# Attention and MLP of one kernel in one hand-written instruction order instead of a scheduler's

## The chip, the cores and the metric

One NeuronCore of a Trainium2 chip runs the whole kernel. Its engines each work through their own list of instructions: PE (TensorE, the matmuls; PEld are its weight loads), DVE (VectorE), ACT (ScalarE), POOL (GpSimd) and SP, which only issues transfers. They wait for each other through semaphores. The metric is the device time of one execution in microseconds (us); lower is better.

## The reference

`B, H, S, D = 4, 8, 768, 48`; `x` has 3072 tokens of 384 values, `d_ff` is 2048.

```python
f = 1.0 / (1.0 + np.exp(-f_logit))
for t in range(S):
    state = f[:, :, t, :, None] * state + np.einsum('bhd,bhe->bhde', k[:, :, t], v[:, :, t])
    y[:, :, t] = np.einsum('bhd,bhde->bhe', q[:, :, t], state)
...
x = np.ascontiguousarray(attn_out.transpose(0, 2, 1, 3)).reshape(B * S, H * D)
h = x @ w_in
h2 = h * h
h3 = h2 * h
P = a[0] + a[1] * h + a[2] * h2 + a[3] * h3
Q = 1.0 + np.abs(b[0]) * np.abs(h) + np.abs(b[1]) * h2
g = P / (Q + 1e-06)
return (g @ w_out).astype(np.float32)
```

## The kernel before

The sequence is cut into 6 chunks `c` of 128 steps. A chunk has 2 units `u`, each of 2 batches with 8 heads, so there are 12 units of attention. After a chunk's two units comes its MLP on 4 x 128 = 512 tokens: 4 groups `g`, each of 4 blocks of 128 hidden values.

**A unit of attention** (`attention`): ACT makes `ef` and `ls` (log of the gate) from `fn`; PE adds them up (`cs`); ACT makes `A` and `Ai`, their exponentials; DVE makes the products `qkp` of `qn` and `kn` with them; PE transposes these (`tp`), ACT copies them out (`qkT`). PE makes the chunk's contribution to the state, `sv`, and in the same PSUM bank the logs' sums `al`; and the scores `sc`, which DVE masks (`scm`). PE adds up `y` from `scm` and from the old state. ACT copies `y` out (`ysb`); DVE renews the state from `sv` (`stmp`, then `state`), except in the last chunk; PE transposes `ysb` (`xps`), and ACT copies that into `xT`, the MLP's input.

**A group of the MLP** (`mlp`): PE makes `hp` in two halves of 12 matmuls, ACT copies each out (`hy`). DVE works on 2048 columns: `z` (absolute value), `w` and `w*z` (the denominator's part); ACT then takes the logarithm (`lq`) and an exponential (`qi`), which makes the reciprocal. DVE makes the numerator `t` in five steps and multiplies it with `qi` into `gall`. When all 4 groups of a chunk are there, PE makes `op`, 4 blocks of 16 matmuls, which ACT copies out (`osb`) and SP sends to memory.

**What sets the order**: the code lists attention and MLP of a chunk one after the other, and a scheduler orders each engine's instructions when the program is built. Each engine then keeps to its list. The transfers of `fn`, `kn` and `qn` are issued on SP, `vn` and the weights (which become bfloat16 on the way) on POOL. PSUM pools: `ps2` and `ps1` for attention, `psh` with two buffers for `hp`, `pso` for `op`.

Of the kernel before, what the change touches and what calls it, by code (L numbers as in the profile page):

```python
# [17 lines left out]
def kernel(  # L18
# [53 lines left out]
    w_pool = ctx.enter_context(tc.tile_pool(name="w_pool", bufs=1))
    a_sb = w_pool.tile([P, 4], F32, name="a_sb")
    nc.sync.dma_start(out=a_sb, in_=bass.AP(tensor=moe_a.tensor, offset=moe_a.offset,
                                            ap=[[0, P]] + list(moe_a.ap)))
    b_sb = w_pool.tile([P, 2], F32, name="b_sb")
    nc.sync.dma_start(out=b_sb, in_=bass.AP(tensor=moe_b.tensor, offset=moe_b.offset,
                                            ap=[[0, P]] + list(moe_b.ap)))
    babs = w_pool.tile([P, 2], F32, name="babs")
    nc.scalar.activation(babs, b_sb, AF.Abs)  # L80

    ld = ctx.enter_context(tc.tile_pool(name="ld", bufs=3))
    at = ctx.enter_context(tc.tile_pool(name="at", bufs=2))
# [3 lines left out]
    ps2 = ctx.enter_context(tc.tile_pool(name="ps2", bufs=1, space=PSUM))  # L87
    ps1 = ctx.enter_context(tc.tile_pool(name="ps1", bufs=1, space=PSUM))
    psh = ctx.enter_context(tc.tile_pool(name="psh", bufs=2, space=PSUM))
    pso = ctx.enter_context(tc.tile_pool(name="pso", bufs=1, space=PSUM))  # L90

    mask = consts.tile([C, C], F32, name="mask")
    make_upper_triangular(nc, mask, 1.0, diag=True)

    loaded = {}

    def load(c, u):
# [5 lines left out]
        for j in range(UB):  # L103
            b = u * UB + j
            for dst, src, eng in ((fn, f_logit, nc.sync), (kn, k, nc.sync),
                                  (qn, q, nc.sync), (vn, v, nc.gpsimd)):
                eng.dma_start(out=dst[:, j],  # L107
                              in_=src[b, :, t0:t0 + C, :].rearrange("h t d -> t h d"))
        loaded[c, u] = (fn, kn, qn, vn)

    w_sb = {}

    def load_weights():
        w_sb["in"] = w_pool.tile_from(moe_w_in.rearrange("(ko ki) n -> ki ko n", ki=P),
                                      dtype=BF16, name="w_in_sb")
        w_sb["out"] = w_pool.tile_from(moe_w_out.rearrange("(ko ki) n -> ki ko n", ki=P),
                                       dtype=BF16, name="w_out_sb")

    unit_no = [0]

    def attention(c, u, xT):

        fn, kn, qn, vn = loaded.pop((c, u))
        qk = qkp[unit_no[0] % NQK]
        ls = lsp[unit_no[0] % NQK]
        unit_no[0] += 1
        st = states[u]
        fl = "p b h d -> p (b h d)"


        ef = at.tile([C, UB, H, D], F32, name="ef")
        nc.scalar.activation(ef.rearrange(fl), fn.rearrange(fl), AF.Exp, scale=-1.0)
        nc.scalar.activation(ls[:, :, :, 0:D], ef, AF.Ln, bias=1.0)

        cs = ps2.tile([C, 2, 512], F32, name="cs", tag="w2")
        for j in range(UB):
            nc.tensor.matmul(cs[:, j, 0:DM].rearrange("p (h d) -> p h d", h=H), U, ls[:, j, :, 0:D],
                             start=True, stop=True)
        A = at.tile([C, UB, H, D], F32, name="A")
        Ai = at.tile([C, UB, H, D], F32, name="Ai")  # L140
        nc.scalar.activation(A.rearrange("p b h d -> p b (h d)"), cs[:, :, 0:DM], AF.Exp, scale=-1.0)
        nc.scalar.activation(Ai.rearrange("p b h d -> p b (h d)"), cs[:, :, 0:DM], AF.Exp, scale=1.0)
        nc.vector.tensor_mul(qk[:, :, 0, :, 0:D], qn, A)  # L143
        nc.vector.tensor_mul(qk[:, :, 1, :, 0:D], kn, Ai)

        qkT = []
        for j in range(UB):
            tp = ps1.tile([P, 2, HP, C], BF16, name="tp", tag="w1")
            for i in range(2):
                for p in range(HP):  # L150
                    nc.tensor.transpose(tp[:, i, p, :],  # L151
                                        qk[:, j, i, 2 * p:2 * p + 2, :].rearrange("t h d -> t (h d)"),
                                        ident)
            t = at.tile([P, 2, HP, C], BF16, name="qkT", bufs=4)
            nc.scalar.copy(t.rearrange("p a b c -> p (a b c)"), tp.rearrange("p a b c -> p (a b c)"))  # L155
            qkT.append(t)


        if c < NC - 1:
            sv = ps1.tile([P, 512], F32, name="sv", tag="w1")  # L160
            svv = sv[:, 0:UB * HP * D].rearrange("p (b h e) -> p b h e", b=UB, h=HP)
            al = sv[:, 448:448 + UB * HP]
            for j in range(UB):
                for p in range(HP):
                    nc.tensor.matmul(al[:, j * HP + p:j * HP + p + 1],
                                     ls[:, j, 2 * p:2 * p + 2, :].rearrange("t h d -> t (h d)"),
                                     ones, start=True, stop=True)
                    for i in range(2):
                        h = 2 * p + i
                        nc.tensor.matmul(svv[64 * i:64 * i + 64, j, p, :],  # L170
                                         qk[:, j, 1, h, :], vn[:, j, h, :],
                                         start=True, stop=True)

        scm = []
        for j in range(UB):
            sc = ps2.tile([C, 2, HP, C], F32, name="sc", tag="w2")
            for p in range(HP):
                for i in range(2):
                    r = slice(64 * i, 64 * i + D)
                    nc.tensor.matmul(sc[:, i, p, :], qkT[j][r, 1, p, :], qkT[j][r, 0, p, :],  # L180
                                     start=True, stop=True)
            m = at.tile([C, 2 * HP, C], BF16, name="scm", bufs=4)
            mb = bass.AP(tensor=mask.tensor, offset=mask.offset,
                         ap=[mask.ap[0], [0, 2 * HP], mask.ap[1]])
# [34 lines left out]
        for j in range(UB):  # L219
# [3 lines left out]
            for kk in range(KD):  # L223
                nc.tensor.transpose(xps[:, kk, :], yf[:, kk * P:(kk + 1) * P], ident)
# [46 lines left out]
    for x in order[:1]:  # L271
        load(*x)
# [42 lines left out]
```

## Time and profile before

| | |
|---|---|
| time, median of 3 runs | 471.98 us (471.62 to 473.34) |
| the profiled execution, its own time | 471.93 us |
| span of its instructions | 469.9 us |
| PE, DVE, ACT busy | 293.4, 257.8, 231.3 us |
| POOL busy | 24.9 us |

Busy times are sums over the whole span, and engines work side by side; so an engine's share says how much room there would be, and not which one sets the end. The span is what lies between the first and the last instruction; 2.03 us of the execution's time lie around it.

### The profile page before, as it was taken

The numbers are of one execution on the slowest core, as the hardware profiler recorded it, in microseconds if no ns is written. First come the engines' busy times: TensorE is split into PE (matmuls) and PEld (weight loads), VectorE is DVE, ScalarE is ACT, GpSimd is POOL, SyncE is SP. The second block draws the span as 40 slices with busy tenths as digits, with TensorE's granted clock in tenths as the row PEclk, the third lists the DMA queues.
The fourth block names the chain that finished last, engine by engine and source line by source line (L and its number), as shares of the span: only waits on it lengthen the run. The fifth ranks groups of instructions, "written<-read, shape, count | busy, mean of one in ns | idle before, by whom it ended". The sixth has DMA issues, their size and how long they took to land.

```text
span 469.9 us, 4398 instructions
## 1 busy us (share of the span) xinstructions
PE 293.4 (62%) x1744; PEld 157.4 (33%) x1744; DVE 257.8 (55%) x290; ACT 231.3 (49%) x252; POOL 24.9 (5%) x36
## 2 busy tenths in 40 slices
PE   0024596459786558786648786738786638785245
PEld 0013432235533234533324543324443225431013
DVE  3021349872239873229883229893228992229950
ACT  1214568744158734248744237744137944148431
POOL 7001000010010001010001010001000000000000
PEclk9999997657768657858656859656959657877659
DMA  9999992317260007060007160003100000000001
GB/s 141 190 159 187 178 131 39 68 33 120 66 86 0 0 1 117 35 84 0 1 1 104 49 81 4 0 0 35 50 1 0 0 0 36 35 0 0 0 17 50
DMA packets 106068, 24.65 MB, mean 52 GB/s; under 512 B 100545, under 2 KB 105665, under 8 KB 106049
## 3 DMA queue, kind: packets, MB, share of 16 engines
q1 hardware_dynamic: 78624, 18.88, 21.5%
q0 software_dynamic: 27424, 5.51, 13.4%
q8 instruction: 13, 0.21, 0.2%
q14 instruction: 7, 0.05, 0.0%
HBM read 25.17 MB, written 4.72 MB: 64 GB/s over the span
## 4 chain that ended last, share of the span: by engine, by line
PE 44%; DVE 29%; ACT 15%; SPq 6%; issue 4%; DMA 2%; DVEq 0%; ACTq 0%
PE op L262 14%; PE hp L238 11%; PE y L194 6%; SPq L107 6%; PE y L198 5%; DVE scm L185 5%; ACT hy L240 4%; DVE gall L258 4%; DVE t L254 4%; DVE w L246 3%; ACT lq L248 3%; DVE t L256 3%; PE sv L170 2%; DVE w L245 2%; DVE t L257 2%
## 5 line engine op out<-in xcount | busy, mean ns | idle before, releaser
L262 PE MATMUL op<-w_out_sb,gall 128*128 128x384 bf16 x384 | 88.7, 387 | 69.0 <-DVE gall L258 64.9
L238 PE MATMUL hp<-xT,w_in_sb 128*128 128x512 bf16 x288 | 92.1, 490 | 19.0 <-ACT hy L240 14.1
L262 PEld LDWEIGHTS <-gall 128*128 128x128 bf16 x384 | 41.1, 111 | 109.5 <-DVE gall L258 72.0
L248 ACT ACTIVATE lq<-w,one_eps 128x2048 f32<-128x2048 bf16 x24 | 48.1, 2005 | 28.1 <-DVE w L246 28.1
L240 ACT CAST hy<-hp 128x1024 bf16<-128x1024 f32 x48 | 48.1, 1007 | 24.7 <-PE hp L238 23.6
L185 DVE TENSOR_TENSOR scm<-sc,mask 128x1024 bf16<-128x1024 f32 x24 | 29.3, 1220 | 53.9 <-PE sc L180 53.8
L238 PEld LDWEIGHTS <-w_in_sb 128*128 128x128 bf16 x288 | 34.8, 121 | 70.4 <-issue 53.8
L250 ACT ACTIVATE qi<-lq 128x2048 bf16<-128x2048 f32 x24 | 46.0, 1915 | 0.3
L194 PE MATMUL y<-vn,scm 128*128 128x48 bf16 x192 | 36.9, 220 | 13.5 <-DVE scm L185 13.5
L202 ACT CAST ysb<-y 128x384 bf16<-128x384 f32 x24 | 10.3, 482 | 69.8 <-PE y L198 66.2
L243 DVE TENSOR_SCALAR z<-hy 128x2048 uint16<-128x2048 uint16 x24 | 16.5, 689 | 41.6 <-ACT hy L240 41.6
L107 POOL DMA_DIRECT2D vn<-in_v_dram x24 | 21.5, 905 | 295.9 <-PE y L198 249.2
L265 ACT COPY osb<-op 128x384 f32<-128x384 f32 x24 | 11.5, 479 | 52.1 <-PE op L262 46.2
L143 DVE TENSOR_TENSOR qkp<-qn,A 128x768 bf16<-128x768 f32 x12 | 11.5, 958 | 44.4 <-DMA qn<-in_q_dram 22.8
L198 PE MATMUL y<-state,qkT 48*128 48x48 bf16 x160 | 35.0, 219 | 0.0
L151 PE MATMUL tp<-ident,qkp 128*128 128x128 bf16 x192 | 18.8, 242 | 25.5 <-ACT qkT L155 16.1
L258 DVE TENSOR_TENSOR gall<-t,qi 128x2048 bf16<-128x2048 bf16 x24 | 29.3, 1220 | 0.6
L256 DVE TENSOR_TENSOR t<-t,hy 128x2048 bf16<-128x2048 bf16 x24 | 29.2, 1218 | 0.1
L254 DVE TENSOR_TENSOR t<-t,hy 128x2048 bf16<-128x2048 bf16 x24 | 29.2, 1217 | 0.0
L246 DVE TENSOR_TENSOR w<-w,z 128x2048 bf16<-128x2048 bf16 x24 | 29.2, 1218 | 0.0
L155 ACT COPY qkT<-tp 128x1024 bf16<-128x1024 bf16 x24 | 24.2, 1009 | 8.1 <-PE tp L151 8.0
L151 PEld LDWEIGHTS <-qkp 128*128 128x128 bf16 x192 | 14.6, 108 | 33.0 <-issue 17.1
(44 smaller groups left out, 293.3 us busy)
## 6 DMA issues: line engine op xcount, KB each, us to landing
fn<-in_f_logit_dram SPq DMA_DIRECT2D x24, 192.0 KB, 4.1
kn<-in_k_dram SPq DMA_DIRECT2D x24, 192.0 KB, 4.1
qn<-in_q_dram SPq DMA_DIRECT2D x24, 192.0 KB, 3.9
out_dram<-osb SPq DMA_DIRECT2D x24, 192.0 KB, 1.9
vn<-in_v_dram POOLq DMA_DIRECT2D x24, 96.0 KB, 3.6
w_in_sb<-in_moe_w_in_dram POOLq DMA_DIRECT2D x1, 1536.0 KB, 12.4
w_out_sb<-in_moe_w_out_dram POOLq DMA_DIRECT2D x1, 1536.0 KB, 22.4
a_sb<-in_moe_a_dram SPq DMA_DIRECT2D x1, 2.0 KB, 2.6
```

The lines of the kernel that those rows point to most:

```text
L107: eng.dma_start(out=dst[:, j], in_=src[b, :, t0:t0 + C, :].rearrange("h t d -> t h d"))
L185: nc.vector.tensor_mul(m, sc.rearrange("s i p t -> s (i p) t"), mb)
L194: nc.tensor.matmul(yv[:, i, j, p, :], scm[j][:, i * HP + p, :], vn[:, j, h, :], start=True, stop=(c == 0))
L198: nc.tensor.matmul(yv[:, i, j, p, :], qkT[j][r, 0, p, :], st[r, j, p, :], start=False, stop=True)
L238: nc.tensor.matmul(hp[:, e, :], w_in_sb[:, kk, m * P:(m + 1) * P], xT[:, kk, :], start=(kk == 0), stop=(kk == KD - 1))
L240: nc.scalar.copy(y[:, hh * 2 * NT:(hh + 1) * 2 * NT], hp.rearrange("p a n -> p (a n)"))
L246: nc.vector.tensor_mul(w, w, z)
L248: nc.scalar.activation(lq, w, AF.Ln, bias=one_eps)
L250: nc.scalar.activation(qi, lq, AF.Exp, scale=-1.0)
L254: nc.vector.tensor_mul(t, t, y)
L258: nc.vector.tensor_mul(gall[:, g * G:(g + 1) * G, :].rearrange("p a n -> p (a n)"), t, qi)
L262: nc.tensor.matmul(op, gall[:, mm, b * C:(b + 1) * C], w_out_sb[:, mm, :], start=(mm == 0), stop=(mm == KF - 1))
```

## The change

The whole body is written anew. The pieces of attention become small functions (`a_ef`, `a_cs`, ... `a_xe`), and so do those of a group (`m_h`, `m_y`, `m_q`, `m_ln`, `m_ex`, `m_p`, `m_g`, and `m_o`, `m_oe` for the output). The scheduler is switched off: each engine keeps the order in which the code names the pieces. After a first part with units 0 to 2, a loop runs over pairs of groups (`n` even and odd); in each pair stand the second half of unit `ku - 1`, the first half of unit `ku`, and two output blocks of the chunk before. The weights are now loaded as float32 on SP, into two buffers, and POOL makes them bfloat16. Several tiles have one buffer instead of two or more, `psh` among them; both `tp` halves become one, and so do the two halves of `ysb` and of `xT`.

```diff
-    psh = ctx.enter_context(tc.tile_pool(name="psh", bufs=2, space=PSUM))
+    psA = ctx.enter_context(tc.tile_pool(name="psA", bufs=1, space=PSUM))
+    psB = ctx.enter_context(tc.tile_pool(name="psB", bufs=1, space=PSUM))
+    psh = ctx.enter_context(tc.tile_pool(name="psh", bufs=1, space=PSUM))
     ps1 = ctx.enter_context(tc.tile_pool(name="ps1", bufs=1, space=PSUM))
     pso = ctx.enter_context(tc.tile_pool(name="pso", bufs=1, space=PSUM))
 
+    ctx.enter_context(tc.manual_schedule())
...
+        sv = ps1.tile([P, 512], F32, name="sv", tag="w1")
...
+            nc.vector.tensor_add(stmp, svf, stv)
+            nc.vector.tensor_mul(stv, stmp, ab)
+
+    def a_x(n):
+        s = at_[n]
+        xps = ps1.tile([P, UB, KD, C], BF16, name="xps", tag="w1")
...
+    def load_w_in(g):
+        t = wst.tile([P, KD, G * P], F32, name="wst")
+        nc.sync.dma_start(out=t, in_=moe_w_in[:, g * G * P:(g + 1) * G * P].rearrange("(ko ki) n -> ki ko n", ki=P))
+        nc.gpsimd.tensor_copy(w_in_sb[:, :, g * G * P:(g + 1) * G * P], t)
...
+    load(1)
...
+    load_w_in(0)
+    load(2)
+    for g in range(1, NG):
+        load_w_in(g)
...
+    a_T(1)
+    a_x(0)
+    a_xe(0)
+    a_Te(1)
+    load(3)
...
+    m_h(0, 0)
+    m_y(0, 0)
+    a_mul(2)
+    m_h(0, 1)
+    m_y(0, 1)
+    a_T(2)
+    m_h(1, 0)
+    a_Te(2)
+    load(4)
+    a_sc(2, 0)
+    a_sc(2, 1)
+    a_sv(2)
+    a_ef(3)
+    a_mask(2, 0)
+    a_mask(2, 1)
+    a_y(2)
+    a_cs(3)
+    load(5)
+    for g in range(NG):
+        load_w_out(g)
+
+
+    for p in range(NGR // 2):
+        ku = p + 3
+        for odd in range(2):
+            n = 2 * p + odd
...
+            m_y(n + 1, 0)
+            m_q(n)
+            if not odd:
+                if prev:
+                    a_ye(ku - 1)
+                m_h(n + 1, 1)
+                if prev:
+                    a_x(ku - 1)
+                if has:
+                    a_exp(ku)
+                if prev:
+                    a_al(ku - 1)
+                    a_xe(ku - 1)
+                m_ln(n)
+                m_ex(n)
+                m_p(n)
+                m_o(c - 1, g)
+                m_y(n + 1, 1)
+                m_h(n + 2, 0)
+                if has:
+                    a_mul(ku)
+                if prev:
+                    a_st(ku - 1)
+                m_oe(c - 1, g)
+                if has:
+                    a_T(ku)
+            else:
+                if has:
+                    a_Te(ku)
+                m_h(n + 1, 1)
+                m_ln(n)
+                m_ex(n)
+                if has:
+                    a_sc(ku, 0)
+                    a_sc(ku, 1)
+                    a_sv(ku)
+                m_p(n)
+                m_o(c - 1, g)
+                m_y(n + 1, 1)
+                m_h(n + 2, 0)
+                if has:
+                    a_mask(ku, 0)
+                    a_mask(ku, 1)
+                if ku + 1 < NUN:
+                    a_ef(ku + 1)
+                m_oe(c - 1, g)
+                if has:
+                    a_y(ku)
+                if ku + 1 < NUN:
+                    a_cs(ku + 1)
+                if ku + 3 < NUN:
+                    load(ku + 3)
+            m_g(n)
+            if last:
+                for b in range(B):
+                    m_o(c, b, range(g * G, (g + 1) * G))
+    for b in range(B):
+        m_oe(NC - 1, b, (nc.scalar, nc.vector)[b % 2])
```

What this does to the lists, at three places. **ACT, before**, at the end of the MLP of chunk 0 (names as above):

```order
L250 ACTIVATE qi<-lq 128x2048 [waits Activation_49]
L202 CAST ysb<-y 128x8x48 [waits PE_49]
L202 CAST ysb<-y 128x8x48
L225 COPY xT<-xps 128x3x128 [waits PE_49]
L141 ACTIVATE A<-cs 128x768 [waits PE_49]
L225 COPY xT<-xps 128x3x128 [waits PE_49]
L142 ACTIVATE Ai<-cs 128x768
```

Before, attention's end (`ysb`, `xT`, `A`) follows the last `qi` of the chunk's MLP.

**ACT, of the change**, in the even half of a loop's pair from chunk 1 on:

```order
L273 CAST hy<-hp 128x1024 [waits DVE_49,PE_49]
L209 CAST ysb<-y 128x2x8x48 [waits PE_49]
L122 ACTIVATE A<-cs 128x768 [waits PE_49]
L122 ACTIVATE Ai<-cs 128x768
L218 ACTIVATE alast<-sv 128x8
L248 COPY xT<-xps 128x2x3x128 [waits PE_49]
L289 ACTIVATE lq<-w,one_eps 128x2048 [waits DVE_49]
L294 ACTIVATE qi<-lq 128x2048 [waits Activation_49]
L273 CAST hy<-hp 128x1024
```

The same pieces now stand inside each pair of groups, and `xT` of unit `ku - 1` stands ahead of `lq` and `qi` of group `n`.

**PE, of the change**, the same half, where `hp` of group `n + 1` ends:

```order
L263 LDWEIGHTS w_in_sb
L263 MATMUL hp<-xT,w_in_sb 128x512
L240 LDWEIGHTS ysb [waits Activation_49]
L240 MATMUL xps<-ident,ysb 128x128 [waits DVE_49]
...
L330 LDWEIGHTS gall
L330 MATMUL op<-w_out_sb,gall 128x384
```

`xps` lies in the bank of `sv` (tag `w1`, one buffer). Its wait for DVE is one for the instruction that reads `sv` last, `stmp`.

**DVE, of the change**, the same half, from the last step of `t`:

```order
L305 TENSOR_SCALAR t<-t,a_sb 128x2048 [waits DVE_49]
L127 TENSOR_TENSOR qkp_102<-qn,A 128x2x8x48 [waits DMAHW3_49,DMAHW2_49,Activation_49]
L128 TENSOR_TENSOR qkp_102<-kn,Ai 128x2x8x48 [waits DMAHW1_49,DMAHW0_49,Activation_49]
L232 TENSOR_TENSOR stmp<-sv,state_107 128x384 [waits PE_49,Activation_49]
L233 TENSOR_TENSOR state_107<-stmp,alast 128x384 [waits DVE_49,PE_49]
L313 TENSOR_TENSOR gall<-t,qi 128x2048 [waits Activation_49]
```

`stmp` of unit `ku - 1` stands behind all of `w` and `t` of group `n` and behind the two products of unit `ku`, which need `A` and `Ai`.

## Rows read from the trace of the kernel before

**Rows 1.** The page: busy time of each engine, share of the span, instructions.

```profile
PE 293.4 (62%) x1744; PEld 157.4 (33%) x1744; DVE 257.8 (55%) x290; ACT 231.3 (49%) x252; POOL 24.9 (5%) x36
```

**Rows 2.** Windows: us; busy of PE, PEld, DVE, ACT, POOL; PEclk; DMA share, GB/s.

```profile
140.00:148.00 8.00, 4.68 (x40) 2.61 (x38) 8.00 (x10) 5.83 (x5) 0.00 (x0) 1.00 0.00 0
...
172.00:180.00 8.00, 6.63 (x39) 3.90 (x39) 4.92 (x6) 3.21 (x6) 1.84 (x2) 0.50 0.47 25
...
180.00:192.00 12.00, 11.51 (x82) 7.17 (x80) 0.96 (x1) 3.78 (x7) 0.00 (x0) 0.91 0.50 116
```

**Rows 3.** Chain that ended last (start, duration, work): each chunk's first `hp`.

```profile
60.86 5.29 PE hp L238 x12
...
132.96 5.17 PE hp L238 x12
...
204.61 5.18 PE hp L238 x12
```

**Rows 4.** Waits: who waits for whom, total us, times, longest.

```profile
DVE scm L185 <- PE sc L180: 53.8, 8, 12.3
...
DVE z L243 <- ACT hy L240: 41.6, 10, 13.1
```

**Rows 5.** Groups by line and shape: busy us, mean ns of one, idle before.

```profile
L248 ACT ACTIVATE lq<-w,one_eps 128x2048 f32<-128x2048 bf16 x24 | 48.1, 2005 | 28.1 <-DVE w L246 28.1
...
L240 ACT CAST hy<-hp 128x1024 bf16<-128x1024 f32 x48 | 48.1, 1007 | 24.7 <-PE hp L238 23.6 <-DVE t L256 1.1
...
L250 ACT ACTIVATE qi<-lq 128x2048 bf16<-128x2048 f32 x24 | 46.0, 1915 | 0.3
...
L246 DVE TENSOR_TENSOR w<-w,z 128x2048 bf16<-128x2048 bf16 x24 | 29.2, 1218 | 0.0
...
L155 ACT COPY qkT<-tp 128x1024 bf16<-128x1024 bf16 x24 | 24.2, 1009 | 8.1 <-PE tp L151 8.0
...
L245 DVE TENSOR_SCALAR w<-z,babs 128x2048 bf16<-128x2048 bf16 x24 | 19.4, 807 | 0.0
...
L243 DVE TENSOR_SCALAR z<-hy 128x2048 uint16<-128x2048 uint16 x24 | 16.5, 689 | 41.6 <-ACT hy L240 41.6
...
L225 ACT COPY xT<-xps 128x384 bf16<-128x384 bf16 x24 | 11.4, 476 | 7.7 <-PE xps L224 7.7
...
L216 DVE TENSOR_TENSOR stmp<-sv,state 128x384 f32<-128x384 f32 x8 | 4.4, 550 | 12.2 <-ACT alast L207 12.2
...
masks.py:66 POOL TENSOR_SCALAR_AFFINE_SELECT mask<-mask 128x128 f32<-128x128 f32 x1 | 0.3, 305 | 0.0
```

**Rows 6.** Timeline of DVE, last group: first and last of six dependent steps.

```profile
446.51 0.81 DVE L253 TENSOR_SCALAR t<-hy,a_sb 128x2048 bf16<-128x2048 bf16 x1
...
451.52 1.22 DVE L258 TENSOR_TENSOR gall<-t,qi 128x2048 bf16<-128x2048 bf16 x1
```

**Rows 7.** Timeline of PE (start, duration, form, count).

```profile
32.20 1.01 PE L151 MATMUL tp<-ident,qkp 128*128 128x128 bf16 x8 [1.10 <-ACT qkT L155]
...
105.34 0.50 PE L224 MATMUL xps<-ident,ysb 128*128 128x128 bf16 x3 [0.95 <-ACT ysb L202]
...
132.96 10.34 PE L238 MATMUL hp<-xT,w_in_sb 128*128 128x512 bf16 x36 [0.86 <-ACT xT L225]
...
149.30 2.72 PE L238 MATMUL hp<-xT,w_in_sb 128*128 128x512 bf16 x6 [1.77 <-ACT hy L240]
...
178.91 1.46 PE L262 MATMUL op<-w_out_sb,gall 128*128 128x384 bf16 x4 [0.41 <-DVE gall L258]
...
184.88 2.76 PE L262 MATMUL op<-w_out_sb,gall 128*128 128x384 bf16 x16 [0.34 <-ACT osb L265]
```

**Rows 8.** DMA queues, window 36 to 48 us: packets, bytes, rate.

```profile
DMA packets 12312, 2.23 MB, mean 186 GB/s; under 512 B 12312, under 2 KB 12312, under 8 KB 12312
```

**Rows 9.** Timeline of DVE: product of unit 1 (chunk 0).

```profile
46.35 0.96 DVE L143 TENSOR_TENSOR qkp<-qn,A 128x768 bf16<-128x768 f32 x1 [3.82 <-ACT A L141]
```

**Rows 10.** Timeline of ACT: the last eviction.

```profile
466.26 0.48 ACT L265 COPY osb<-op 128x384 f32<-128x384 f32 x1 [2.89 <-PE op L262]
```

More of the change, by code (lines that the diff above doesn't have):

```diff
@@ L109, in load @@
[L109 to L127, printed above, removed]
+                              in_=src[u * UB + j, :, t0:t0 + C, :].rearrange("h t d -> t h d"))
@@ L153, in attention @@
                                         ident)
[L154 to L172, printed above, removed]
@@ L268 @@
[L268 to L284 removed]
+                    nc.tensor.matmul(s["svv"][64 * i:64 * i + 64, j, p, :],
+                                     s["qk"][:, j, 1, h, :], s["vn"][:, j, h, :],
+                                     start=True, stop=True)
@@ new lines, in a_sc, with a_mask @@
+    def a_sc(n, j):
+        s = at_[n]
+        sc = (psA, psB)[j].tile([C, 2, HP, C], F32, name="sc", tag="AB"[j])
+        for p in range(HP):
+            for i in range(2):
+                r = slice(64 * i, 64 * i + D)
+                nc.tensor.matmul(sc[:, i, p, :], s["qkT"][r, j, 1, p, :], s["qkT"][r, j, 0, p, :],
+                                 start=True, stop=True)
+        s["sc", j] = sc
+    def a_mask(n, j):
+        s = at_[n]
+        m = at.tile([C, 2 * HP, C], BF16, name=f"scm{j}")
+        mb = bass.AP(tensor=mask.tensor, offset=mask.offset,
+                     ap=[mask.ap[0], [0, 2 * HP], mask.ap[1]])
+        nc.vector.tensor_mul(m, s["sc", j].rearrange("s i p t -> s (i p) t"), mb)
+        s["scm", j] = m
@@ new lines, in a_y, with mm @@
+    def a_y(n):
+        s = at_[n]
+        y = psA.tile([C, 2, 512], F32, name="y", tag="A")
+        yv = y[:, :, 0:DM].rearrange("t i (b p e) -> t i b p e", b=UB, p=HP)
+        first = [True, True]
+        def mm(j, p, i, lhsT, rhs):
+            nc.tensor.matmul(yv[:, i, j, p, :], lhsT, rhs, start=first[i], stop=True,
+                             skip_group_check=True)
+            first[i] = False
+        heads = [(j, p, i) for j in range(UB) for p in range(HP) for i in range(2)]
+        if s["c"] > 0:
+            for j, p, i in heads:
+                r = slice(64 * i, 64 * i + D)
+                mm(j, p, i, s["qkT"][r, j, 0, p, :], s["st"][r, j, p, :])
+        for j, p, i in heads:
+            mm(j, p, i, s["scm", j][:, i * HP + p, :], s["vn"][:, j, 2 * p + i, :])
+        s["y"] = yv
@@ new lines, with m_h @@
+    xTs, galls, mg = {}, {}, {}
+    NGR = NC * NG
+    def m_h(n, half):
+        if n >= NGR:
+            return
+        c, g = divmod(n, NG)
+        hp = psh.tile([P, 2, NT], F32, name="hp", tag="h")
+        xT = xTs[c].rearrange("p k b t -> p k (b t)")
+        for e in range(2):
+            m = g * G + half * 2 + e
+            for kk in range(KD):
+                nc.tensor.matmul(hp[:, e, :], w_in_sb[:, kk, m * P:(m + 1) * P], xT[:, kk, :],
+                                 start=(kk == 0), stop=(kk == KD - 1))
+        mg.setdefault(n, {})["hp", half] = hp
@@ new lines @@
+    a_ef(0)
+    a_cs(0)
+    a_exp(0)
+    a_mul(0)
+    a_T(0)
+    a_ef(1)
+    a_cs(1, psh)
+    a_Te(0)
+    a_sc(0, 0)
+    a_sc(0, 1)
+    a_sv(0)
+    a_exp(1)
+    a_mask(0, 0)
+    a_mask(0, 1)
+    a_al(0)
+    a_y(0)
+    a_mul(1)
+    a_ye(0)
+    a_st(0)
+    a_T(1)
[3 more added lines that the diff above has]
+    load(3)
+    nc.scalar.activation(babs, b_sb, AF.Abs)
+    a_sc(1, 0)
+    a_sc(1, 1)
+    a_sv(1)
+    a_ef(2)
+    a_mask(1, 0)
+    a_mask(1, 1)
+    a_al(1)
+    a_y(1)
+    a_cs(2)
```

342 lines of the change are left out of this document (192 added, 150 removed).

## The prediction, as it was made before the change was run

> **What bounds the kernel now.** I read the busy times first: no engine is busy for two thirds of the span [rows 1]. So I look at windows. In the MLP DVE is busy for 8.00 us of 8; in the attention that follows it is busy for 0.96 of 12, while PE works 11.51 [rows 2]. The two stages alternate: a chunk lasts from one first `hp` to the next, 204.61 - 132.96 = 71.65 us [rows 3], and DVE's waits say the same, 53.8 us for the scores and 41.6 us for the next chunk's `hy` [rows 4]. Half a chunk (two groups, one unit, two output blocks, which is what a pair of the new loop holds) costs 35.8 us. DVE's own work in it is at most 257.8 / 12 = 21.5 us [rows 1]. The most that weaving can give is the difference, 14.3 us per pair.
>
> **DVE's list in a pair.** The old list mixes `w` with `t` and so hides the end of each instruction behind an independent one; the new one is a chain. The last group of the old kernel shows what a chain costs: five steps of `t`, from 446.51 to 451.52, 5.01 us [rows 6]. The first three of a group take 0.69 + 0.81 + 1.22 [rows 5], with the gap of 0.03 that those rows have: 2.78 to the end, 2.68 until the independent `t` may start (rows of independent neighbours overlap by some 0.1). With t's last step also followed by something independent (-0.15) `t` ends at 2.68 + 4.85 = 7.5 us after the group's start. **Odd half:** 7.5, two masks and `gall`, each 1.22 long and 1.14 apart, make 10.9 us. **Even half, if nothing stalls:** 7.5, two products (0.96 each [rows 9], 0.9 apart), `stmp` and `state` (0.55 each, a chain: 1.1), `gall` 1.1, so 11.5 us. Together 22.4 us.
>
> **The wait that comes with it.** In the even half `xps` of unit `ku - 1` must wait for `stmp`, since it overwrites `sv` in the single buffer of `ps1`, and `stmp` stands on DVE behind `w`, `t` and both products. Queued behind `xps` on PE are `op`, the next `hp` and `tp`; behind `xT` on ACT are `lq` and `qi` of group `n`, for which DVE's `gall` waits. From the group's start: the products begin at 7.5, `stmp` at 9.3, its end 9.85 (0.55) [rows 5]. Six transposes after an idle PE: three took 0.50 [rows 7], three more at 0.11 each: 10.7. `xT` now has 768 columns; between 476 ns for 384 and 1009 for 1024 [rows 5] that is 0.80: 11.5. `lq` 2.0 and `qi` 1.9: 15.45. `gall` then takes 15.5 to 16.7, and `z` of the odd half follows at 16.6; its `hy`, which ACT makes straight after `qi` (1.0), is there at 16.4. So the even half costs 16.6 us instead of 11.5, and the pair 16.6 + 10.9 = 27.5; with a few hand-overs between engines I take 27.7.
>
> In the odd half all must be ready in time. PE: `hp` needs that `hy` (16.4) and takes 1.3 us (24 of the matmuls of [rows 7]'s 36 in 10.34 - 5.17 = 5.17, so 0.215 each) or 2.7 (six in 2.72). `tp`, 16 transposes, 1.7 at the slow rate (eight took 1.01 in an early row [rows 7]) and about half at the fast one. ACT: `hy`, then `qkT` of 2048 columns, 1.0 + 0.85 = 1.85: at 20.6 or 22.7. `lq` and `qi` then end at 24.5 or 26.6; `gall` has its place at 26.4. It fits within 0.2 us either way. The first half of unit `ku + 1` (`y`, `ysb`, `A`, `Ai`) is done some 4 us before the next pair's products ask for it, if PE is fast in the odd half.
>
> **PE's clock.** In a window with a granted clock of 0.50 (1.2 GHz) four matmuls of `op` took 1.46; in the next, with PE busy throughout and 0.91 (mostly 2.4 GHz), 16 took 2.76 [rows 2, 7]. In a pair PE is idle before `xps` and then busy almost without a break from 9.9 to 29, so I take it as slow at first and fast for the odd half.
>
> **The start.** The loads come with 8 x 1024 packets for a unit (4 tensors, 2 batches, one packet of at most 192 bytes per step and head); 12312 packets went in 12 us [rows 8], so a unit takes 8.0 us. Unit 0 lies in memory at 11 us (I allow 3 us until data flow) and unit 1 at 19. A quarter of `w_in`, 0.8 MB in larger packets, would need 4.2 us at that window's 186 GB/s; I take 3.2: the first at 22, unit 2 at 30, the rest at 40, units 3 to 5 at 64, `w_out` at 77. Unit 1's products, behind unit 0's masks on DVE, start at 21.6: `ef` of unit 1 (its `fn`, first in line beside `vn`, at 15) stands before `qkT` of unit 0 on ACT, 16.7 to 18.6, then scores and two masks of 1.2. From unit 1's products to the first `hp` the old kernel took 60.86 - 46.35 = 14.5 us [rows 3, 9], with the same steps in the same order; so 36.1. Then the new order has `hp`, `hy`, `hp`, `hy` (2.7 + 1.0 twice), `tp` 1.7, another `hp` 2.7, eight scores (no longer than transposes; I take 0.6) and two masks 2.4 before group 0: 50.9 if PE is slow throughout, 46 if fast. I take 49.5.
>
> **The casts of the weights** on POOL have no row. A POOL row that reads and writes 128 float columns took 0.305 us [rows 5]; 1536 columns are between that (all fixed cost) and 12 times that, 3.7 us. The eight casts have some 8 us of slack or more (the second quarter of `w_in` is in memory at 33 and wanted by the third `hp` at 44; `w_out` at 77, wanted in the third pair, 49.5 + 2 x 27.7 + 10 = 115), so I put them at nothing; without that cover each late cast would shift the start by its length.
>
> **The sum.** Start 49.5. Eight pairs with the wait (units 2 to 9 have a state to renew): 8 x 27.7 = 221.6. The ninth pair has no `stmp` and so no wait: 7.5 + 1.8 + 1.1 + 10.9 = 21.3. Three pairs without attention: 6 x (7.5 + 1.15) = 51.9. In the last chunk PE also makes that chunk's own `op` in parts, behind each `gall`, 16 + 16 + 12 matmuls per group, 8 us of 8.65 if fast; I add 1.5. The end: 16 matmuls at 2.76 to 5.8 (four times 1.46), I take 4.2; then `osb` and its transfer, 469.9 - 466.26 = 3.6 [rows 10]. In all 353.6, and with the 2.0 us that lay around the span 355.6: **356 us** (the profiled execution, 471.93, is the median of before within 0.1). Moving `y`'s state matmuls together, the merged copies and fewer `xps` waits save PE and ACT time that isn't on this path: nothing.
>
> **Rivals.**
> (1) *DVE alone sets the pair.* If the wait for `stmp` cost nothing, a pair would be 22.4: 8 x 5.3 = 42 us less, 314. For it: all other work fits. Against it: the wait stands in the list, and `lq` can't pass `xT`. 0.06.
> (2) *PE stays slow in the odd half.* Then 23 us of PE work follow `hy` at 16.4 (three times `hp` 2.7, `tp` 1.7, scores 1.2, `op` 5.2 to 5.8, and by estimate, at 0.05 to 0.1 for a small matmul, 5 for `sv`, `y` and `cs`, and waits), and `A` and `Ai` come 3 us too late for the products: pairs of 30.7, and some 5 us in the last chunk, 385. For it: the clock was 0.50 over a whole window in which PE was busy for 6.63 of 8 us [rows 2]. Against: PE has hardly a break here. 0.17. The Trainium skill ("TensorE: Matmul & The Clock Gate", "HAM oscillation") tells of kernels whose clock falls in each wait for data; by it this is what happens, with the same price.
> (3) *The weave does not overlap.* If ACT's fixed order makes each pair as long as half an old chunk, 35.8, it is 8 x 8.1 = 65 us more: 421. For it: each engine now blocks on its first unready instruction. Against: the list above, step by step. 0.03.
> (4) *POOL's casts hold DVE up.* If DVE stood still while POOL works, the four casts of `w_out`, which fall into the first pairs, would cost up to 4 x 3.7 = 15 us: 371. For it: they meet a busy DVE. Against: DVE has 5 us of idle time in each of these pairs. 0.06. The Trainium skill ("SBUF — State Buffer", "Who interferes with whom") says that GpSimd and a DVE instruction with two inputs or in a two-port mode lock each other out for a whole instruction; no row here shows such a case.
> (5) *The casts come late, and it is slower.* `op` of the first chunk, which PE's list holds ahead of all later `hp`, needs all of `w_out`. To lose the 116 us, the last cast must end 116 us after 115, at 231; from the first at 22 that is 26 us for each of eight, 7 times the upper bound. 0.02.
> The forecast has 0.66 with its own range of 346 to 368 (start 45 to 54, pairs 27.2 to 28.5).
>
> **Range and chances.** 342 to 387 holds the forecast with some room, (4), and most of (2), 0.83. A change of 0.5% is about what this measurement can tell from none. Faster by more 0.97, within 0.01, slower 0.02.
>
> **What would show it.** Right: `xps` waits for DVE's `stmp` in eight pairs, for about 5 us; `gall` in the even half waits for `qi` for some 5 us; DVE is 80% busy in the loop; groups in the last three pairs are 8.7 us apart. Wrong: DVE without gaps (1), `qkp` waiting for `A` (2), DVE's instructions longer beside POOL's copies (4), copies over 10 us (5), or a first `z` far from 50 us.

## The result and the profile after

The changed kernel takes 358.72 us (median of 4 runs, 357.12 to 360.75), the kernel before 472.66 us: a ratio of 0.759, 95% interval 0.754 to 0.764. That is 114 us less, and 2.7 us more than the 356 us predicted. The profiled execution took 357.51 us with a span of 355.2 us.

Two rows of its page, busy times and the chain that ended last by engine:

```profile
PE 206.3 (58%) x1722; PEld 113.1 (32%) x1744; DVE 273.3 (77%) x290; ACT 224.2 (63%) x214; POOL 37.0 (10%) x42
...
DVE 63%; ACT 15%; issue 7%; DMA 7%; PE 5%; SPq 2%; DVEq 0%; ACTq 0%
```

Against [rows 1] DVE does a little more work (273.3 us against 257.8) in a much shorter span. PE's busy time fell by 87 us, some because `y` is cheaper and some because its clock is up more often, but PE holds only 5% of the chain. The waits (who waits for whom: total us, times, longest):

```profile
ACT xT L248 <- PE xps L240: 67.2, 10, 9.0
PE xps L240 <- DVE stmp L232: 60.1, 8, 8.9
...
DVE gall L313 <- ACT qi L294: 39.2, 8, 4.9
...
DVE scm L182 <- PE sc L173: 16.4, 3, 6.9
```

The two big waits of [rows 4] (53.8 us for the scores, 41.6 us for `hy`) have shrunk to 16.4 us for the scores, all before the loop, and none for `hy`. In their place stands the wait that was forecast, eight times, once per pair with a state to renew. Timeline of DVE, first some rows of the first two pairs, then the pair from 160.15 to 187.91:

```profile
66.37 2.37 DVE L302 TENSOR_TENSOR t<-t,hy 128x2048 bf16<-128x2048 bf16 x1
68.77 1.84 DVE L303 TENSOR_SCALAR t<-t,a_sb 128x2048 bf16<-128x2048 bf16 x1
...
75.97 1.96 DVE L280 TENSOR_SCALAR z<-hy 128x2048 uint16<-128x2048 uint16 x1
...
160.15 0.68 DVE L280 TENSOR_SCALAR z<-hy 128x2048 uint16<-128x2048 uint16 x1
...
169.73 0.55 DVE L232 TENSOR_TENSOR stmp<-sv,state 128x384 f32<-128x384 f32 x1
...
175.84 1.23 DVE L313 TENSOR_TENSOR gall<-t,qi 128x2048 bf16<-128x2048 bf16 x1 [4.90 <-ACT qi L294]
176.98 0.69 DVE L280 TENSOR_SCALAR z<-hy 128x2048 uint16<-128x2048 uint16 x1
...
187.91 0.69 DVE L280 TENSOR_SCALAR z<-hy 128x2048 uint16<-128x2048 uint16 x1
```

PE and ACT in the same pair, and ACT's last output tile:

```profile
170.33 0.80 PE L240 MATMUL xps<-ident,ysb 128*128 128x128 bf16 x6 [7.92 <-DVE stmp L232]
170.93 4.68 PE L330 MATMUL op<-w_out_sb,gall 128*128 128x384 bf16 x16
```

```profile
171.17 0.80 ACT L248 COPY xT<-xps 128x768 bf16<-128x768 bf16 x1 [8.08 <-PE xps L240]
171.86 2.00 ACT L289 ACTIVATE lq<-w,one_eps 128x2048 f32<-128x2048 bf16 x1
173.90 1.91 ACT L294 ACTIVATE qi<-lq 128x2048 bf16<-128x2048 f32 x1
...
350.87 0.48 ACT L340 COPY osb<-op 128x384 f32<-128x384 f32 x1 [2.01 <-DMA out_dram<-osb]
```

From these rows one reads the chain in order: `stmp` ends at 170.28, `xps` starts, `xT` 171.17, `lq`, `qi`, and only then, at 175.84, can DVE make `gall`. `w`, the input of `lq`, had been ready since 163.3. DVE stood still for 4.90 us in a pair of 27.76.

### The profile page after: what moved, and what is told of

It is laid out like the page before. It is cut to its first block, busy times and chain, and to the rows that moved or that the text cites. A ratio compares the mean times of both kernels' runs of the same rounds, so it can differ in the third digit from the quotient of the medians.

```text
span 355.2 us, 4363 instructions
## 1 busy us (share of the span) xinstructions
PE 206.3 (58%) x1722; PEld 113.1 (32%) x1744; DVE 273.3 (77%) x290; ACT 224.2 (63%) x214; POOL 37.0 (10%) x42
## 4 chain that ended last, share of the span: by engine, by line
DVE 63%; ACT 15%; issue 7%; DMA 7%; PE 5%; SPq 2%; DVEq 0%; ACTq 0%
DVE gall L313 8%; DVE t L302 7%; DVE w L283 7%; DVE t L304 7%; DVE w L282 6%; ACT lq L289 5%; DMA kn<-in_k_dram 5%; DVE t L303 5%; DVE z L280 5%; ACT qi L294 4%; DVE scm L182 4%; DVE t L301 4%; DVE t L305 3%; DVE qkp L128 3%; DVE qkp L127 2%
## 5 line engine op out<-in xcount | busy, mean ns | idle before, releaser
L263 PE MATMUL hp<-xT,w_in_sb 128*128 128x512 bf16 x266 | 76.7, 412 | 53.1 <-ACT hy L273 50.0
L330 PE MATMUL op<-w_out_sb,gall 128*128 128x384 bf16 x384 | 80.1, 371 | 5.6 <-DVE gall L313 5.6
L263 PEld LDWEIGHTS <-w_in_sb 128*128 128x128 bf16 x288 | 29.7, 103 | 90.0 <-issue 68.0
L248 ACT COPY xT<-xps 128x768 bf16<-128x768 bf16 x12 | 9.6, 803 | 67.2 <-PE xps L240 67.2
L240 PE MATMUL xps<-ident,ysb 128*128 128x128 bf16 x72 | 9.1, 291 | 60.3 <-DVE stmp L232 60.1
L182 DVE TENSOR_TENSOR scm<-sc,mask 128x1024 bf16<-128x1024 f32 x24 | 28.2, 1217 | 16.4 <-PE sc L173 16.4
L240 PEld LDWEIGHTS <-ysb 128*128 128x128 bf16 x72 | 7.1, 128 | 64.7 <-issue 62.3
L144 ACT COPY qkT<-tp 128x2048 bf16<-128x2048 bf16 x12 | 22.4, 1869 | 0.1
L282 DVE TENSOR_SCALAR w<-z,babs 128x2048 bf16<-128x2048 bf16 x24 | 20.9, 870 | 0.9
L303 DVE TENSOR_SCALAR t<-t,a_sb 128x2048 bf16<-128x2048 bf16 x24 | 19.3, 803 | 0.8
L301 DVE TENSOR_SCALAR t<-hy,a_sb 128x2048 bf16<-128x2048 bf16 x24 | 19.4, 807 | 0.0
```

The costliest lines, as they stand in the source:

```text
L182: nc.vector.tensor_mul(m, s["sc", j].rearrange("s i p t -> s (i p) t"), mb)
L263: nc.tensor.matmul(hp[:, e, :], w_in_sb[:, kk, m * P:(m + 1) * P], xT[:, kk, :], start=(kk == 0), stop=(kk == KD - 1))
L282: nc.vector.tensor_scalar(w, z, babs[:, 1:2], babs[:, 0:1], op0=ALU.mult, op1=ALU.add)
L303: nc.vector.tensor_scalar(t, t, a_sb[:, 1:2], None, op0=ALU.add)
L330: nc.tensor.matmul(ops[c, b], galls[c][:, mm, b * C:(b + 1) * C], w_out_sb[:, mm, :], start=(mm == 0), stop=(mm == KF - 1))
```

## The experiments

All are edits of the changed kernel unless another is named; times are medians, ratios are to the kernel before on the same chip.

**1. The state update early.** The one edit takes the forecast wait away by making `stmp` before `xps` asks for it:

```diff
             m_y(n + 1, 0)
+            if prev and not odd:
+                a_al(ku - 1)
             m_q(n)
             if not odd:
                 if prev:
+                    a_st(ku - 1)
                     a_ye(ku - 1)
...
-                    a_al(ku - 1)
                     a_xe(ku - 1)
...
-                if prev:
-                    a_st(ku - 1)
```

> In each pair, alast of the previous unit (ScalarE) moves to right behind the even group's last copy hy, and the state update stmp, state (VectorE) to right behind the even group's last product of the w chain, ahead of both qkp. Nothing is added or left out. Theory of the prediction: the transposes xps wait for stmp, that wait passes through xT, lq and qi to gall, and costs each of the 8 woven pairs about 5 us. Then xps no longer waits for stmp (60 us of waits in all become under 10), gall's wait for qi goes from 4.9 us to under 1, a pair goes from 27.8 to 22.5 to 23.5 us, and the time from 358.7 to 318 to 326 us. Rival, that something else sets the pair (ScalarE's or TensorE's own chain): the wait moves to another releaser of gall, the pair stays at 27 to 28 us, and the time within 354 to 362.

Measured: 316.42 us, ratio 0.669 (0.667 to 0.671). Timeline of DVE, one pair, and one row of the waits:

```profile
140.48 0.69 DVE L280 TENSOR_SCALAR z<-hy 128x2048 uint16<-128x2048 uint16 x1
141.20 0.93 DVE L282 TENSOR_SCALAR w<-z,babs 128x2048 bf16<-128x2048 bf16 x1
...
143.31 0.55 DVE L232 TENSOR_TENSOR stmp<-sv,state 128x384 f32<-128x384 f32 x1
...
150.99 1.22 DVE L313 TENSOR_TENSOR gall<-t,qi 128x2048 bf16<-128x2048 bf16 x1
...
163.06 0.69 DVE L280 TENSOR_SCALAR z<-hy 128x2048 uint16<-128x2048 uint16 x1
```

```profile
PE xps L240 <- DVE stmp L232: 12.4, 8, 2.6
```

`gall` no longer waits at all, and the pair is 163.06 - 140.48 = 22.58 us, the 22.4 us of rival (1), which is DVE's list without a stall. So the wait for `stmp` set the pair: the edit only moves `alast`, `stmp` and `state`, and eight pairs fell from 224.6 to 184.4 us, 40 of the 42 us that the time fell.

**2. `y` alternating again.**

```diff
-        if s["c"] > 0:
-            for j, p, i in heads:
-                r = slice(64 * i, 64 * i + D)
-                mm(j, p, i, s["qkT"][r, j, 0, p, :], s["st"][r, j, p, :])
         for j, p, i in heads:
             mm(j, p, i, s["scm", j][:, i * HP + p, :], s["vn"][:, j, 2 * p + i, :])
+            if s["c"] > 0:
+                r = slice(64 * i, 64 * i + D)
+                mm(j, p, i, s["qkT"][r, j, 0, p, :], s["st"][r, j, p, :])
```

> The matmuls of y alternate again between the one on the scores and the one on the state, as in the kernel before; everything else is as in the changed kernel. Theory of the prediction: y is off the path in a pair, since the VectorE chain ends last and y's copy waits behind hy on ScalarE; y takes some 4 us longer on TensorE (about 4.9 in place of 0.9), of which nothing to 1 us comes through per pair, so the time is 357 to 366. Rival: the regrouping is what shortens the pair; then 8 pairs lose 4 us each and the time is about 390.

Measured: 363.97 us, ratio 0.770 (0.768 to 0.771); 5.2 us more. A middle pair lasts as long as before (160.60 to 188.25, 27.65 us). The loss is in two places, the even halves after the last two units, where no `stmp` follows (DVE's timeline):

```profile
283.49 1.23 DVE L312 TENSOR_TENSOR gall<-t,qi 128x2048 bf16<-128x2048 bf16 x1 [2.93 <-ACT qi L293]
...
305.35 1.23 DVE L312 TENSOR_TENSOR gall<-t,qi 128x2048 bf16<-128x2048 bf16 x1 [2.17 <-ACT qi L293]
```

Their sum, 5.1 us, is the loss. In the eight pairs the slower `y` disappears in the time in which `xps` waits anyway.

**3. The same with the state early** (edits 1 and 2 together).

> The state update early, as in the run with the early state, and y's matmuls alternating again. In the changed kernel y's 4 us cost nothing in the 8 woven pairs because xps had to wait for stmp anyway. Theory: with that wait gone, y's longer run delays hp, xps, xT, lq and qi, and gall then waits for qi: 1.4 to 3 us in each of 8 pairs, and 5 us in the last two units as before, so 332 to 346 against 316.4. Rival, that y is off the path for another reason: 5 us at the end alone, 320 to 323.

Measured: 336.99 us, ratio 0.711 (0.707 to 0.716), 20.6 us more than experiment 1. With the cover gone, eight pairs take 199.2 us against 184.4, and what lies between them and the last `gall` is 4.6 us longer. So in the changed kernel it was the wait for `stmp` that hid `y`. The time lies in the expected range, but `y` comes through in two ways, and only one had been expected. DVE's timeline in one pair:

```profile
104.66 0.56 DVE L232 TENSOR_TENSOR state<-stmp,alast 128x384 bf16<-128x384 f32 x1 [2.41 <-PE y L193]
...
113.06 1.22 DVE L312 TENSOR_TENSOR gall<-t,qi 128x2048 bf16<-128x2048 bf16 x1 [1.07 <-ACT qi L293]
```

`gall`'s waits for `qi` (0.7 to 1.5 us in six of the eight pairs) are 6.9 us. In five pairs `state`, which experiment 1 put further ahead, itself waits for `y`, which reads the old state that it overwrites: 7.8 us in all. The early place has this price of its own where `y` is slow.

**4. `y` grouped in the kernel before**, the same regrouping as the only edit there (the flags that start an accumulation change with the order).

> The kernel before with one edit of the change alone: y's matmuls on the state all stand ahead of those on the scores, where they alternated. In the kernel before y stood on the chain that ended last, in 12 steps of about 4.9 us, of which the regrouped form needs about 1. Theory: up to 3.9 us for each of 10 to 12 steps, so the time falls from 473 to 427 to 445. Rival, that something beside it (copies on ScalarE) takes the place of y: 460 to 473.

Measured: 440.36 us, ratio 0.930 (0.927 to 0.934), 33 us less. Groups by line, of the kernel before and of this one:

```profile
L194 PE MATMUL y<-vn,scm 128*128 128x48 bf16 x192 | 36.9, 220 | 13.5 <-DVE scm L185 13.5
...
L198 PE MATMUL y<-state,qkT 48*128 48x48 bf16 x160 | 35.0, 219 | 0.0
```

```profile
L193 PE MATMUL y<-vn,scm 128*128 128x48 bf16 x192 | 9.6, 212 | 2.9 <-DVE scm L185 2.9
...
L193 PE MATMUL y<-state,qkT 48*128 48x48 bf16 x160 | 4.9, 207 | 10.6 <-DVE scm L185 10.6
```

One matmul lasts 0.21 to 0.22 us either way; what differs is how far the next one overlaps it. The clock does not explain it: one `y` of each kernel, looked at in windows, ran at a granted clock of 0.50 (196.4 to 201.2 us before, 164.5 to 165.7 us here). The same edit is worth 33 us in the kernel before, 5 in the changed one and 21 with the state early: an edit has no price of its own, only one beside what else stands on the path.

**5. No weave.** The same pieces and merged copies in a hand-written order, but each chunk's two units stand ahead of its four groups:

```diff
-    for p in range(NGR // 2):
-        ku = p + 3
...
+    for c in range(NC):
+        units_of(c)
...
+        for g in range(NG):
...
             m_p(n)
             m_o(c - 1, g)
```

> The same pieces in a hand-written order, with nothing woven: at the head of each chunk stand the two attention units of that chunk, the second one step behind the first, and then the four MLP groups alone; only the output blocks of the chunk before stay between the groups. Merged copies, early state matmuls of y, early loads of w_out and no planner, as in the changed kernel. Theory: the gain comes from attention and MLP lying side by side. Without that a chunk costs about 62 to 65 us (71.8 in the kernel before, less some 4 us for each of its two y), and the time is 395 to 430. Rival, that most of the gain comes from the other edits: 360 to 380.

Measured: 428.69 us, ratio 0.904 (0.898 to 0.910). DVE's timeline, the first group of two chunks:

```profile
118.71 0.69 DVE L280 TENSOR_SCALAR z<-hy 128x2048 uint16<-128x2048 uint16 x1 [8.44 <-ACT hy L273]
...
184.57 0.69 DVE L280 TENSOR_SCALAR z<-hy 128x2048 uint16<-128x2048 uint16 x1 [9.71 <-ACT hy L273]
```

A chunk takes 65.9 us, against 71.65 [rows 3] and two pairs of 27.7 = 55.4. So, in this order of adding them, some 45 of the 114 us come from the edits beside the weave (`y` is probably the largest, by experiment 4, which is in another kernel), and 70 from the weave, although its own list stalls DVE in each pair.

**6. TensorE kept busy** in front of `xps` in six pairs:

```diff
                 if prev:
+                    if 2 <= p <= 7:
+                        m_fill(c - 1, g)
                     a_x(ku - 1)
```

> In 6 of the pairs, 36 extra matmuls are put on TensorE ahead of xps, into the bank that the op matmuls then start afresh, so that TensorE works while xps would wait and its granted clock is up when xps and the even half's op come; the output stays the same. Theory: TensorE's clock in that stretch is not on the path, apart from xps (0.8 us slow against about 0.5 fast); the even half's op takes about 2.8 us in place of 4.7, and the time falls by 0 to 3 us. Rival, that the slow clock sets the pair: 2 us or more of each of 6 pairs, 12 us or more in all. If the fill matmuls themselves delay xps, the time grows by what xps then waits for TensorE.

Measured: 356.37 us, ratio 0.754 (0.751 to 0.756), 2.3 us less, an interval that touches the changed kernel's. PE's timeline:

```profile
166.31 6.01 PE L322 MATMUL op<-w_out_sb,gall 128*128 128x384 bf16 x36
172.81 0.49 PE L240 MATMUL xps<-ident,ysb 128*128 128x128 bf16 x6 [0.49 <-DVE stmp L232]
173.14 2.76 PE L337 MATMUL op<-w_out_sb,gall 128*128 128x384 bf16 x16
```

`op` takes 2.76 us where it took 4.68, and six pairs together are only 1.2 us shorter (164.9 against 166.1). The first of the six is 1.3 us longer, since there the added matmuls end 1.7 us after `stmp` and hold `xps` up; the other five are 0.3 to 0.6 us shorter. Of that, 0.3 is `xps` (0.49 us in place of 0.80); the rest is a step of `w` that POOL no longer lengthens (told below). So the slow `op` was not on the path, and the slow `xps` was, with 0.3 us a pair.

**7. The casts of `w_out` twice.**

```diff
         nc.gpsimd.tensor_copy(w_out_sb[:, g * G:(g + 1) * G, :], t)
+        nc.gpsimd.tensor_copy(w_out_sb[:, g * G:(g + 1) * G, :], t)
```

> Each of the four GpSimd casts of w_out is done twice, with the same result. Theory of the lock between GpSimd and VectorE: each cast lengthens one VectorE instruction by 1.1 to 1.3 us, as it did to four of them in the first two pairs; eight casts lengthen up to eight, so the time grows by 2 to 5 us, and the first two pairs show it. Rival, that those instructions were long for another reason (DMA writes into the same memory): the number of long ones stays at four and the time within 1 us of 358.7.

Measured: 361.49 us, ratio 0.764 (0.762 to 0.766). That interval overlaps the changed kernel's, so the trace decides. POOL's timeline in the changed kernel, and DVE's with the casts doubled:

```profile
65.91 1.75 POOL L352 CAST w_out_sb<-wst 128x1536 bf16<-128x1536 f32 x1 [16.72 <-DMA wst<-in_moe_w_out_dram]
68.14 1.92 POOL L352 CAST w_out_sb<-wst 128x1536 bf16<-128x1536 f32 x1 [0.48 <-DMA wst<-in_moe_w_out_dram]
...
```

```profile
67.01 2.36 DVE L302 TENSOR_TENSOR t<-t,hy 128x2048 bf16<-128x2048 bf16 x1
69.41 1.84 DVE L303 TENSOR_SCALAR t<-t,a_sb 128x2048 bf16<-128x2048 bf16 x1
```

The `t` steps at 66.37 and 68.77 in the changed kernel take 2.37 and 1.84 us, beside these two casts; in the pair from 160.15 the same steps take 1.23 and 0.76. So a cast lengthens the DVE instruction beside it by 1.1 to 1.3 us. There are three such instructions in the changed kernel (the third is `z` at 75.97), and with the casts doubled seven, longer by 0.7 to 1.2 us; the one cast of each kernel without one lies beside `scm`, which has one of its inputs in PSUM. The first two pairs take 63.0 us against 58.5.

**8. State first, and other steps to go below experiment 1.**

```diff
+            if prev and not odd:
+                a_al(ku - 1)
+                a_st(ku - 1)
             m_q(n)
...
         nc.vector.tensor_scalar(z.bitcast(U16), y.bitcast(U16), 0x7FFF, None, op0=ALU.bitwise_and)
+        if early:
+            nc.vector.tensor_scalar(t, y, a_sb[:, 3:4], a_sb[:, 2:3], op0=ALU.mult, op1=ALU.add)
         nc.vector.tensor_scalar(w, z, babs[:, 1:2], babs[:, 0:1], op0=ALU.mult, op1=ALU.add)
+        if early:
+            nc.vector.tensor_mul(t, t, y)
         nc.vector.tensor_mul(w, w, z)
...
-        osb = ms.tile([P, DM], F32, name="osb")
+        osb = ms.tile([P, DM], F32, name="osb", bufs=4)
```

> Three edits on the changed kernel. The previous unit's stmp and state stand first on VectorE in the even group, ahead of z, and its alast right behind the copy hy. In the 18 groups that have attention beside them the steps of t and of w alternate, so that fewer instructions follow directly on the one that makes their operand (a dependent one starts about 0.03 us after the end of the other, an independent one about 0.08 us before it). The output tile has 4 buffers in place of 2. Theory: the pair is now VectorE's own sum, so 4 dependences less in each of 18 groups give 0.4 to 0.5 us each, 7 to 9 us; the output tiles' wait at the end gives 2 to 4 us; together 303 to 309 us. Rival, that the order of VectorE's instructions is worth nothing: 312 to 316.

Measured: 327.43 us, ratio 0.692 (0.690 to 0.694). Both my theory and its rival missed: it is 11 us slower than experiment 1. DVE's timeline, then ACT's:

```profile
172.93 0.56 DVE L232 TENSOR_TENSOR stmp<-sv,state 128x384 f32<-128x384 f32 x1 [2.41 <-ACT alast L218]
```

```profile
171.80 1.01 ACT L273 CAST hy<-hp 128x1024 bf16<-128x1024 f32 x1
172.71 0.19 ACT L218 ACTIVATE alast<-sv 128x8 f32<-128x8 f32 x1
```

By its row `stmp` itself waits for `alast`, though it doesn't use its result. Both read the tile `sv`; the likely reason, which no run tests, is that the program puts these two reads in order. So all of DVE, with `z` next in line, stood for 2.4 us behind a 0.19 us instruction that stands late on ACT, behind `hy` of the next group. In experiment 1 `alast` was in the same place, but three instructions of `z` and `w` stood in front of `stmp`.

**9. The state between.** The alternating steps and the four output tiles of experiment 8 stay; `alast` stands in the odd group behind `qi`, `stmp` behind the first step of `w`, `state` behind `w`:

```diff
                     a_sv(ku)
+                    a_al(ku)
                 m_p(n)
...
         nc.vector.tensor_scalar(w, z, babs[:, 1:2], babs[:, 0:1], op0=ALU.mult, op1=ALU.add)
+        if u is not None:
+            a_stmp(u)
...
         nc.vector.tensor_mul(w, w, z)
+        if u is not None:
+            a_state(u)
```

> As the run before it (steps of t and w alternating in 18 groups, output tile with 4 buffers), but alast of a unit stands on ScalarE right behind qi of the odd group in which sv is made, and no longer behind the next group's hy; on VectorE stmp stands behind z, the first step of t and the first of w of the even group, and state behind the last product of w. Theory: what cost the earlier run its 11 us was that stmp, first on VectorE, stood in front of z and waited 2.4 to 2.5 us in each pair for alast; with alast made some 4 us earlier that wait is gone and the even group keeps its 9.95 us and 1.1 us for the state, the odd one its 10.4, together 21.5 in place of 22.5 us: 305 to 310 us. Rival, that the alternation itself makes lq late and gall waits: 316 to 327.

Measured: 306.37 us, ratio 0.648 (0.644 to 0.651). DVE's timeline:

```profile
136.58 0.68 DVE L290 TENSOR_SCALAR z<-hy 128x2048 uint16<-128x2048 uint16 x1
137.18 0.81 DVE L292 TENSOR_SCALAR t<-hy,a_sb 128x2048 bf16<-128x2048 bf16 x1
...
157.84 0.69 DVE L290 TENSOR_SCALAR z<-hy 128x2048 uint16<-128x2048 uint16 x1
```

The pair is 21.26 us, 1.3 less than in experiment 1: the alternation was right, and the places of `alast` and the state were what had failed. Both moved here. On ACT `alast` now runs at 135.19 for 0.16 us, so it is done 1.2 us before the group's first `z` at 136.58. By that `stmp` at the very front would not have waited for it either; no run has that order.

**10. `w_out` cast by its transfers**, on top of experiment 9.

```diff
-        t = wst.tile([P, G, DM], F32, name="wst")
-        nc.sync.dma_start(out=t, in_=moe_w_out[...])
-        nc.gpsimd.tensor_copy(w_out_sb[:, g * G:(g + 1) * G, :], t)
+        nc.gpsimd.dma_start(out=w_out_sb[:, g * G:(g + 1) * G, :], in_=moe_w_out[...])
```

> As the run with the state between, but w_out is turned to bf16 by its four transfers, issued by GpSimd, and not by four GpSimd casts. Theory of the lock: without the casts no VectorE instruction of the first two pairs is lengthened by 1.1 to 1.3 us, which saves 2 to 4 us, less what the issue of the transfers on GpSimd lengthens. Rival, that the issue on GpSimd or the transfers' traffic costs as much as the casts (qn and vn then come late): 0 to 5 us slower than that run.

Measured: 303.48 us, ratio 0.641 (0.639 to 0.642), the fastest version here: 55 us below the changed kernel. The first two pairs take 44.3 us against 47.0 in experiment 9. POOL's timeline shows what replaces the casts, and no DVE instruction of the first two pairs is lengthened by more than 0.3 us any more:

```profile
50.34 2.99 POOL L364 DMA_DIRECT2D w_out_sb<-in_moe_w_out_dram  x4
```

## Why the prediction was right, and where its terms were off

**The wait: right in mechanism and size.** Predicted from the group's start: products at 7.5, `stmp` 9.3, `xT` done 11.5, `qi` done 15.45, next `z` 16.6. Measured in the pair above: 7.84, 9.58, 11.82, 15.66 and 16.83; 0.3 of this is one step of `w` at 1.12 in place of 0.81 us; it stands beside POOL's issue of `vn` (160.63 to 162.47), as it does in four pairs. Pairs three to eight average (270.90 - 104.82) / 6 = 27.68 us, as summed. That the wait, and not DVE's work, makes it 27.7 is shown by experiment 1. The ninth pair, without `stmp`, took 21.34 (21.3). Of the signs, DVE was 80% busy (133.53 of 166.08 us in pairs three to eight) and `gall` waited 4.90 us; but `xps` waited 7.5 us on average (60.1 in eight), not 5: PE ran out of other work sooner than forecast. That changes nothing in the pair, which hangs on when `stmp` ends.

**PE's clock: right.** Windows of the changed kernel (us; busy of PE, PEld, DVE, ACT, POOL; PEclk; DMA share, GB/s):

```profile
165.00:170.00 5.00, 0.00 (x0) 0.00 (x0) 4.89 (x7) 0.00 (x0) 0.00 (x0) 0.50 1.21 178
170.00:175.00 5.00, 4.67 (x20) 2.52 (x20) 0.84 (x2) 3.80 (x3) 0.00 (x0) 0.52 0.00 0
...
180.00:188.00 8.00, 6.87 (x98) 4.01 (x98) 7.86 (x9) 7.94 (x8) 0.00 (x0) 1.00 0.00 0
```

PE is idle, then runs at the lower level (0.52), and is at full clock in the odd half (1.00), where rival (2) needed it slow. Experiment 6 prices the slow stretch at 0.3 us a pair. It also made some of the odd half slow (six matmuls of `hp` 2.03 and `tp` 1.91 us, in place of 1.46 and 1.06), and its pairs were no longer for it; a slow odd half as a whole, rival (2), no run shows. The Trainium skill ("TensorE: Matmul & The Clock Gate", "HAM oscillation") tells of a matmul kernel whose clock falls in each wait for data. The rows agree on the fall (0.50 in the window without PE work); but the section has the work behind the wait start slow, not stay slow, so it gives rival (2) less support than the prediction took from it.

**The casts: "I put them at nothing" was the step that failed**, by about 3 us. I weighed whether a cast would come late, and it doesn't; but while it works, DVE's instruction stands. The first two pairs took 29.67 and 28.85 us, 3.1 more than forecast, and experiments 7 and 10 show the cause from both sides: with twice the casts these pairs grew by 4.5 us, without casts they shrank by 2.7 (from experiment 9 to 10). Rival (4) named the mechanism and put its bound at 15 us; a cast takes 1.6 to 1.9 us, and holds DVE for at most 1.3 of it. The Trainium skill ("SBUF — State Buffer", "Who interferes with whom") has this as an exclusive lock for a whole instruction; the rows agree (`t` with two inputs 1.14 us longer, `z` with one 1.27). Each of the three long instructions ends within 0.2 us of the time at which its cast ends plus its own usual length (the first: 65.91 + 1.75 + 1.23 = 68.89, measured 68.74), as if it had stood until the cast was done.

**`y` grouped saves nothing: right in the eight pairs, wrong in the last two units**, where it saves 5.2 us (experiment 2). The step looked at the pair with the wait alone.

**The start, 49.5, was 46.30.** First `hp` at 35.44 (forecast 36.1); from there PE was fast (granted clock 1.00) and not between slow and fast: 46 was the fast end. **The last three pairs, 51.9 and 1.5 more for PE, were 53.31 in all**: a group takes 8.87 us and not 8.65, since there `t`'s last step is followed by the `gall` that needs it, so nothing of it is hidden; PE's parts of `op` cost nothing. **The end, 7.8, was 9.65 us**: with two output tiles the last copies wait 2.0 us for a transfer each (the last row of ACT above), which the old kernel's end did not show me. With four tiles (experiment 8) it was 7.05, but there the last `op` also took 2.77 us in place of 4.37; experiment 1, with two tiles and `op` at 2.77, took 8.36, so the tiles are worth about 1.3. Together: -3.2, +3.1, -0.1, +1.85, and the span came out 1.6 us above its sum. That the total is so close is in part luck: the start and the casts, each wrong by 3 us, cancel.

## What to carry to other kernels

In a hand-written order, look for each instruction that takes over a buffer, and ask what must have read it and where that reader stands in its own engine's list: here 0.55 us of work in the wrong place cost 42 of 359 us. Price an edit beside the stalls that remain, since a stall hides other work until it is gone (`y`: 5 us, then 21). And moving the culprit to the very front did not cure it: what it waits for, `alast`, still stood late (327 us; 306 once both had other places).

## What the hardware showed that I had not expected

Matmuls of `y` on 48 rows and on 128 rows that alternate start 0.13 us apart (granted clock 1.00, experiment 2) to 0.15 us (0.50, kernel before), and grouped 16 of them end in 0.37 to 0.58 us. PE's timeline, experiment 2 and then the changed kernel:

```profile
160.05 0.20 PE L193 MATMUL y<-vn,scm 128*128 128x48 bf16 x1
160.18 0.19 PE L193 MATMUL y<-state,qkT 48*128 48x48 bf16 x1
...
164.48 2.77 PE L262 MATMUL hp<-xT,w_in_sb 128*128 128x512 bf16 x6
```

```profile
159.45 0.37 PE L193 MATMUL y<-state,qkT 48*128 48x48 bf16 x16
159.75 0.58 PE L193 MATMUL y<-vn,scm 128*128 128x48 bf16 x16
...
160.96 1.46 PE L263 MATMUL hp<-xT,w_in_sb 128*128 128x512 bf16 x6 [0.30 <-ACT hy L273]
```

The `hp` behind is slower too: in experiment 2 PE was busy for all of 159.8 to 163.8 at a granted clock of 1.00, and from 163.8 to 167.3 the clock was 0.51. So here the clock fell without a gap in the rows of PE. The Trainium skill ("TensorEngine Tiling (Array Packing)", "Key Properties") says that a change of the tiling mode drains TensorE; the rows fit that, but no run here tells it from another cause, such as that alternating matmuls add to the same columns of PSUM one right behind the other.

On DVE the order of the same instructions is worth something: `w` directly behind the `z` that it needs starts 0.03 us after its end (141.20 behind 140.48 + 0.69), an independent one 0.08 before it (137.18 against 136.58 + 0.68). In the odd half experiments 1 and 9 have the same DVE instructions in another order, and it takes 10.43 us in place of 10.93. The even half is 0.8 shorter; of that, 0.1 is a step of `w` that POOL's issue of `vn` lengthened in experiment 1 (0.93 us) and does not here.
